# Wk's first load moves to ScalarE's DMA queue, and one transpose moves up, at the start of a two-layer transformer kernel

## The chip, the cores and the metric

The kernel runs on one core of a Trainium2 chip. A core has five engines that run side by side, each with its own instruction stream: TensorE (PE in the profile; its weight loads are PEld), VectorE (DVE), ScalarE (ACT), GpSimd (POOL) and SyncE (SP). They share an on-chip memory (SBUF) and an accumulation memory (PSUM), and wait for each other by semaphores. Sixteen DMA engines move data; SyncE, ScalarE and GpSimd can each issue transfers on a queue of their own. The metric is the device time of one execution in microseconds (us), as the median of several.

## What is computed

Two layers over 2048 tokens of 1024 features (bf16), the same weights in both: attention over eight keys at distances 0, 2, ..., 14, with 32 heads of 32 features, and a feed-forward part of 3584 hidden features. Each part stands behind a layer norm and is added to its input.

```python
def _A_ref(x, wqkv, wo):
    qkv = (x @ wqkv).reshape(B, S, 3, H, Dh).transpose(2, 0, 3, 1, 4)
    q, k, v = qkv[0], qkv[1], qkv[2]
    idx = pos[:, None] - (jnp.arange(8) * 2)[None, :]
    ...
    logits = jnp.where(mask, einsum("bhsd,bhswd->bhsw", q, kg) * scale, -1e9)
    o = einsum("bhsw,bhswd->bhsd", softmax(logits), vg)
    return o.transpose(0, 2, 1, 3).reshape(B, S, D) @ wo

def _B_ref(x, w1, b1, w2, b2):
    return gelu(x @ w1 + b1) @ w2 + b2

x = x + _A_ref(_layernorm(x), A_wqkv, A_wo)
x = x + _B_ref(_layernorm(x), B_w1, B_b1, B_w2, B_b2)
# and both lines once more
```

## The kernel before

The tokens are cut into four groups of 512 (four tiles of 128 tokens each), so that two layers make eight stages `n` = 0 to 7. A stage runs `gen_qkv` (queries, keys, values), the attention itself on VectorE (`new_prod`, `logits`, `weights`, `av`), `gen_wo` (output projection), `gen_ffn1` and `gen_ffn2`. The calls at the end of the kernel interleave the generators by hand; TensorE's order is the order in which they are written (`pe` chains every matmul to the one before). `InOrder` does the same for the other engines where its `on` flag is set. SyncE's flag is set from the load of group 1's first two tiles until the end of the first early layer norm, ScalarE's during the start of stage 0.

What matters here is the start of stage 0. The weights wqkv are loaded in three parts of 2 MB: Wq, Wk and Wv. Wk and Wv come as two halves of 1 MB each (`load_qkv`); the first Wq comes as eight rows of 256 KB (`load_wq_row`), shared out between the queues of SyncE and ScalarE together with the first four tiles of x. All weight halves share a ring of five buffers (`wpool`).

Stage 0 treats its first two token tiles unlike the others. TensorE transposes raw x of tiles 0 and 1 before the layer norm is known, and multiplies it with Wq row by row (`queries_of_raw`: for each row `k`, seven column chunks `c`, with an eighth chunk at the end); the norm is put in afterwards (`finish`, on VectorE and GpSimd). While this runs, `rest` computes the norm of tiles 2 and 3: VectorE's statistics (`stats`), a square root on ScalarE (`root`), then the normalised tiles (`norm`). Tiles 2 and 3 are transposed on TensorE between the rows, through one PSUM bank: tile 2 after place (6, 6), that is row 6, chunk 6, and tile 3 after place (7, 6); ScalarE copies each out of the bank (`transpose_on_pe`, `copy_transposed`). Tiles 0 and 1 are normalised as well, and their transposes for keys and values are done by two DMA transposes on SyncE.

After the rows TensorE computes the queries of tiles 2 and 3, then the keys of the whole group (eight chunks of eight matmuls; the first four use Wk's first half and the last four its second), then the values. SyncE issues in this order: tile 0 of x, Wq rows 0, 2, 3, tile 3, rows 5, 6, 7, group 1's tiles 0 and 1, the two DMA transposes, Wk's first half, group 1's tile 2, Wk's second half, group 1's tile 3, the four tiles of group 2, then the transposes of the early layer norm (`ln_early`) of group 1, and Wv. ScalarE issues tiles 1 and 2 and rows 1 and 4.

`ln_early` norms group 1 and the first tile of group 2 on VectorE, in two parts (two tiles, then three); `ln_stats_ahead` computes the statistics of the other tiles of group 2 on ScalarE and GpSimd during the keys.

Of the kernel before, what the change touches and what calls it, by code (L numbers as in the profile page):

```python
# [17 lines left out]
def kernel(  # L18
# [19 lines left out]
    _, S, D = A_x.shape  # L38
# [12 lines left out]
    KD = D // P  # L51
# [10 lines left out]
    wqkv_v = A_wqkv.rearrange("(k p) f -> p k f", p=P)  # L62
# [15 lines left out]
    def acc_tile():  # L78
        return psum.tile([P, T], F32, name="acc", bufs=8)
# [23 lines left out]
    vec, act, pool, sp = InOrder(nc.vector), InOrder(nc.scalar), InOrder(nc.gpsimd), InOrder(nc.sync)  # L103
# [17 lines left out]
    def load_x(g, t0=0, t1=NTT, engine=None):  # L121
        for tt in range(t0, t1):
            t = g * NTT + tt
            (engine or sp).dma_start(x[t][:], x_in[t * P:(t + 1) * P, :])

    def load_qkv(which, between=None, behind=None):
        tiles = []
        for h in range(2):
            wt = wpool.tile([P, KD // 2, D], BF16, name="wt")
            load = sp.dma_start(wt[:], wqkv_v[:, h * (KD // 2):(h + 1) * (KD // 2), which * D:(which + 1) * D])  # L130
            if h == 0 and behind:
                tc.add_manual_dep(load.ins, behind.ins.name,
                                  mybir.DependencyInfo(mybir.DependencyClass.Sync, mybir.DependencyReason.DATA),
                                  reason="behind the spread of the weights")
            if h == 0 and between:
                between()
            tiles.append(wt)
        return tiles

    def load_wq_row(k, engine):  # L140
        engine.dma_start(wq_first[k // (KD // 2)][:, k % (KD // 2), :], wqkv_v[:, k, 0:D])
# [3 lines left out]
    for k in (0, 2, 3):  # L145
        load_wq_row(k, sp)
    load_x(0, 3, 4)
    for k in range(5, KD):
        load_wq_row(k, sp)

    warm = bigp.tile([P, P], BF16, name="big")
# [8 lines left out]
    load_x(0, 1, 2, act)  # L160
    load_wq_row(1, act)
    load_x(0, 2, 3, act)
    load_wq_row(4, act)
    act.on = False
    ident = const.tile([P, P], BF16, name="ident")
    make_identity(nc, ident[:])
# [66 lines left out]
    def copy_transposed(out, bank, parts):  # L233
        pst = bank[:].bitcast(BF16).rearrange("p (k t) -> p k t", t=P)
        for k0, k1 in zip(parts[:-1], parts[1:]):
            act.copy(out[:, k0:k1, :], pst[:, k0:k1, :])
# [11 lines left out]
    def ln_first():  # L248

        xnT = xa[0] = new_xnT()  # L250
        vec.on = act.on = True
        raw = attp.tile([P, KD, NT + 2], BF16, name="vT", bufs=2)
        vec.memset(raw[:, :, NT:NT + 2], 1.0)
        mv = lnp.tile([P, 4, 2], F32, name="mvs", bufs=1)
        std = lnp.tile([P, 4], F32, name="stds", bufs=1)
        rstd = lnp.tile([P, 4], F32, name="rstds", bufs=1)
        less = lnp.tile([P, 2], F32, name="lesses", bufs=1)

        def stats(tt):
            st6 = lnp.tile([P, 2, 6], F32, name="stats")  # L260
            for h in range(2):
                vec.bn_stats(st6[:, h, :], x[tt][:, h * HALF:(h + 1) * HALF])
            vec.bn_aggr(mv[:, tt, :], st6[:])

        def root(t0, t1):
            act.activation(std[:, t0:t1], mv[:, t0:t1, 1], ACT.Sqrt, bias=eps_t[:])

        def norm(tt, out):
            if tt > 1:
                vec.reciprocal(rstd[:, tt:tt + 1], std[:, tt:tt + 1])  # L270
            vec.tensor_scalar(out=out, in0=x[tt][:], scalar1=mv[:, tt, 0:1], scalar2=rstd[:, tt:tt + 1],
                              op0=ALU.subtract, op1=ALU.mult)
            return out

        warm_ps = acc_tile()
        warm_up(7, warm_ps)
        banks = [acc_tile(), acc_tile()]
        for tt in range(2):
            transpose_on_pe(x[tt], raw[:, :, tt * P:(tt + 1) * P], banks[tt], (0, 2))
        warm_up(2, warm_ps)  # L280
        for tt in range(2):
            copy_transposed(raw[:, :, tt * P:(tt + 1) * P], banks[tt], (2, KD))
            stats(tt)
        root(0, 2)
        vec.tensor_scalar(out=less[:], in0=mv[:, 0:2, 0], scalar1=-1.0, scalar2=None, op0=ALU.mult)
        vec.reciprocal(rstd[:, 0:2], std[:, 0:2])
        by_token = iop.tile([P, 4, P], F32, name="tmp")

        def spread_stats(bank):
            for i, column in enumerate((less[:, 0:1], less[:, 1:2], rstd[:, 0:1], rstd[:, 1:2])):  # L290
                pe(nc.tensor.transpose(bank[:, i * P:(i + 1) * P], column.to_broadcast([P, P]), identf[:]))
            rows = by_token[:].rearrange("p i t -> p (i t)")
            act.copy(rows, bank[:])
            return rows[:, 0:NT], rows[:, NT:2 * NT]

        xn01 = bigp.tile([P, 2, D], BF16, name="big")

        def rest():
            for tt in range(2, 4):
                stats(tt)  # L300
                root(tt, tt + 1)
            for tt in range(2, 4):
                xn = lnp.tile([P, D], BF16, name="xn", bufs=3)
                norm(tt, xn[:])
                first_late.append((xn, xnT[:, tt, :, :]))
            for tt in range(2):
                first_early.append((norm(tt, xn01[:, tt, :]), xnT[:, tt, :, :]))

        return raw, spread_stats, rest

    def queries_of_raw(wq, qT):
        raw, spread_stats, rest = st.pop("raw")
        first = {}

        def row(c, k):
            if k == 0:
                first[c] = acc_tile()
            mm(first[c][:, 0:NT + 2], lhsT=wq[k // (KD // 2)][:, k % (KD // 2), c::NCH], rhs=raw[:, k, :],
               start=(k == 0), stop=(k == KD - 1), skip_group_check=True)

        part = attp.tile([P, NCH, NT], F32, name="abc")

        def finish(c):
            vec.scalar_tensor_tensor(out=part[:, c, :], in0=less, scalar=first[c][:, NT:NT + 1], in1=first[c][:, 0:NT],
                                     op0=ALU.mult, op1=ALU.add)
            pool.tensor_tensor(out=qT[:, c, 0:NT], in0=part[:, c, :], in1=rstd, op=ALU.mult)

        for k in range(KD):
            for c in range(7):
                row(c, k)  # L330
                if (k, c) == (0, 6):
                    bank = acc_tile()
                if (k, c) == (2, 6):
                    less, rstd = spread_stats(bank)
                    rest()
                if (k, c) == (6, 6):
                    transpose_on_pe(*first_late.pop(0), bank)
                if (k, c) == (7, 6):
                    transpose_on_pe(*first_late.pop(0), bank, (0, KD // 2, KD))
        act.on = False  # L340
        act.hold()
        for c in range(7):
            finish(c)
        for k in range(KD):
            row(7, k)
        vec.on = False
        return lambda: finish(7)

    def new_xnT(pool=None):
        return (pool or xnp).tile([P, NTT, KD, P], BF16, name="xnT")  # L350
# [38 lines left out]
    def gen_qkv(n, defer=False, qk_pool=None, v_late=False, qk_next=None, v_first=False, mix=0):  # L389
# [5 lines left out]
        if v_first:  # L395
            wv = load_qkv(2)
        wq = wq_first if n == 0 else load_qkv(0)
        if n > 0 and not v_first:
            wk = load_qkv(1, behind=last_spread[0] if n == 2 else None)
# [15 lines left out]
        if v_first:  # L415
            yield from values()
            wk = load_qkv(1)
        qT = qk_pool.tile([P, NCH, T], BF16, name="qT")
        if n == 0:
            last = queries_of_raw(wq, qT)  # L420
            for xn, out in first_early:
                sp.dma_start_transpose(out, xn.rearrange("s (k p) -> s k p", p=P))
            wk = load_qkv(1, lambda: load_x(1, 2, 3))
            load_x(1, 3, 4)
            load_x(2)
            early_tiles = ln_early((1, None), (2, qk_next))
            next(early_tiles)
            last()
            next(early_tiles)
            wv = load_qkv(2)  # L430
            for _ in early_tiles:
                pass
            vec.hold()
            sp.on = False
            sp.hold()
# [89 lines left out]
    def between(n, m):  # L525

        vec.on = True
        for c in range(2):
            new_prod(m, c, False)
        add_prods(m, 0)  # L530
        logits(n)
        add_prods(m, 1)
        weights(n)
        spread(n)
        new_prod(m, 2, False)
        add_prods(m)
        vec.on = False
# [101 lines left out]
    def warm_up(count, ps):  # L639
        for _ in range(count):  # L640
            mm(ps[:], lhsT=warm[:], rhs=warm[:].unsqueeze(1).to_broadcast([P, NTT, P]), start=True, stop=True)
# [135 lines left out]
```

## Time and profile before

| what | us |
|---|---|
| median of 5 executions | 1231.26 (1230.96 to 1231.49) |
| the profiled execution's own time | 1231.26 |
| its span, first to last instruction | 1229.5 |
| VectorE busy | 865.0 |
| ScalarE busy | 315.8 |
| DMA, mean rate | 185 GB/s |

Busy time is the time in which an engine ran an instruction of the kernel; DMA issues don't count. In a row of a timeline stand the start, the duration, the engine (a q behind it means its sequencer, which issues DMAs), the source line, the operation, the tile written and the tiles read, the shapes and the number of instructions merged into the row; in brackets the idle time of the engine ahead of it and what ended that. Nearly all rows have line L92 or L117, since helpers on those lines record every operation; the tile names tell them apart: `wt` is a weight half, `x` a token tile, `raw` (shown as vT) the raw transposed tiles, `xn` and `big` normalised tiles, `xnT` transposed ones, `acc` a PSUM bank. A row of a table by stretches has the stretch, its length, the busy time (and number of instructions) of PE, PEld, DVE, ACT and POOL, the granted clock, the share in which the DMA engines were busy, and their rate in GB/s.

The chain of waits that ended last goes, in its first part, through the loads of x and VectorE's statistics:

```profile
17.38 8.21 DMA x<-in_A_x_dram
25.58 0.02 issue
25.61 1.30 DVE stats L92 x2
```

### The profile page before, as it was taken

Reading aid. Unit: us, or ns where it says so; the run is one execution under the profiler, and the core shown is the slowest. Engines: PE = TensorE matmul, PEld = TensorE weight load, DVE = VectorE, ACT = ScalarE, POOL = GpSimd, SP = SyncE. Lnnn points to the kernel's source line nnn. Section 1 sums busy time; section 2 is a strip of 40 time slices with the busy share of each in tenths; the row PEclk is TensorE's granted clock in tenths of the full one; section 3 lists DMA queues with packets and bytes.
Section 4 is the critical chain, followed back from the end, with each engine's and each line's share of the span. In section 5 each row is a group of like instructions: output and inputs, shape, how many; then the busy total and the mean of one; then the engine's idle time right before and its main releaser. Section 6 shows DMA issues by size and latency. Waiting matters only on the chain.

```text
span 1229.5 us, 13975 instructions
## 1 busy us (share of the span) xinstructions
PE 1221.0 (99%) x5719; PEld 632.9 (51%) x5769; DVE 865.0 (70%) x922; ACT 315.8 (26%) x497; POOL 127.6 (10%) x220
## 2 busy tenths in 40 slices
PE   9999999999999999999999999999999999999998
PEld 7666544456444564445544465444654444444444
DVE  7999898998997999375993759937599797011001
ACT  4543253014410144202441024410244001400310
POOL 2630006010101101100001000010000002000000
PEclk9999999999999999999999999999999999999999
DMA  8966665766647645856447565476664568446441
GB/s 278 296 206 184 183 206 184 201 169 205 213 136 240 186 154 166 236 170 181 155 159 233 171 171 176 158 219 202 171 200 145 187 195 209 148 159 196 156 136 50
DMA packets 225824, 227.18 MB, mean 185 GB/s; under 512 B 74000, under 2 KB 192928, under 8 KB 223712
## 3 DMA queue, kind: packets, MB, share of 16 engines
q1 hardware_dynamic: 216304, 208.17, 56.1%
q0 software_dynamic: 8880, 17.07, 4.0%
q8 instruction: 45, 0.74, 0.3%
q10 hardware_dynamic: 576, 1.05, 0.2%
q14 instruction: 19, 0.16, 0.0%
HBM read 189.01 MB, written 4.19 MB: 157 GB/s over the span
## 4 chain that ended last, share of the span: by engine, by line
PE 90%; DVE 5%; POOL 1%; DMA 1%; issue 1%; ACT 0%; SPq 0%; DVEq 0%
PE acc L117 90%; DVE big L92 4%; POOL rstd_ahead L92 1%; DMA x<-in_A_x_dram 1%; DVE e L92 0%; DMA abc<-a 0%; POOL mv_ahead L92 0%; DVE tmp L92 0%; DVE stats L92 0%; DVE oT L92 0%; PE acc L230 0%; DVE abc L92 0%; SPq L92 0%; POOL abc L92 0%; ACT xn L92 0%
## 5 line engine op out<-in xcount | busy, mean ns | idle before, releaser
L117 PE MATMUL acc<-xnT,wt 128*128 128x512 bf16 (+1 forms) x3328 | 713.2, 377 | 1.3 <-DMA wt<-in_A_wqkv_dram 1.3
L117 PEld LDWEIGHTS <-wt 128*128 128x128 bf16 x3392 | 400.7, 119 | 319.7 <-DMA wt<-in_A_wqkv_dram 1.7
L117 PE MATMUL acc<-wt,hT 128*128 128x512 bf16 (+1 forms) x1780 | 386.0, 376 | 2.1
L117 PEld LDWEIGHTS <-hT 128*128 128x128 bf16 x1820 | 178.1, 98 | 208.9
L92 DVE TENSOR_TENSOR big<-big 128x2048 bf16<-128x2048 bf16 (+2 forms) x185 | 245.2, 1355 | 2.2
L92 ACT ACTIVATE hT<-acc,b1T 128x512 bf16<-128x512 f32 x224 | 151.8, 689 | 323.7 <-PE acc L117 323.6
L92 DVE TENSOR_TENSOR big<-qT,kT 128x4096 bf16<-128x4096 bf16 x64 | 144.0, 2287 | 37.2 <-ACT kT L92 35.9
L92 DVE TENSOR_TENSOR big<-abc,vT 128x4096 bf16<-128x4096 bf16 x64 | 144.8, 2288 | 9.9 <-DMA abc<-a 7.4
L92 DVE TENSOR_TENSOR tmp<-acc,b2bc 128x512 f32<-128x512 f32 x56 | 38.7, 691 | 156.1 <-PE acc L117 152.9
L92 ACT CAST qT<-acc 128x512 bf16<-128x512 f32 (+1 forms) x64 | 35.6, 558 | 278.7 <-PE acc L117 277.0
L117 PE MATMUL acc<-wt,oT 128*128 128x512 bf16 x440 | 97.6, 379 | 0.4
L92 DVE BATCH_NORM_STATS2 stats<-x 128x6 f32<-128x512 bf16 x114 | 76.3, 682 | 7.2 <-DMA x<-in_A_x_dram 6.2
L117 PEld LDWEIGHTS <-oT 128*128 128x128 bf16 x448 | 43.8, 98 | 53.0 <-DVE oT L92 0.3
L92 DVE TENSOR_TENSOR x<-acc,big 128x512 bf16<-128x512 f32 (+1 forms) x9 | 5.7, 632 | 90.0 <-PE acc L117 90.0
L92 POOL TENSOR_TENSOR rstd<-mv,eps_t 128x1 f32<-128x1 f32 x48 | 14.6, 304 | 501.1 <-DVE mv L92 501.1
L92 ACT CAST vT<-acc 128x512 bf16<-128x512 f32 x64 | 37.4, 585 | 100.1 <-PE acc L117 100.1
L92 ACT CAST kT<-acc 128x512 bf16<-128x512 f32 x64 | 37.0, 585 | 59.9 <-PE acc L117 59.9
L92 DVE TENSOR_TENSOR x<-acc,x 128x512 bf16<-128x512 f32 x64 | 43.0, 671 | 4.9 <-PE acc L117 4.6
L92 DVE TENSOR_SCALAR xn<-x,mv,rstd 128x1024 bf16<-128x1024 bf16 x48 | 26.2, 547 | 19.9 <-POOL rstd L92 19.9
L92 DVE TENSOR_TENSOR x<-tmp,x 128x512 bf16<-128x512 f32 x56 | 38.7, 691 | 1.4
L92 POOL DMA_DIRECT2D big<-big x24 | 13.3, 564 | 212.3 <-DVE big L92 212.3
L92 ACT ACT_TABLE_LOAD x17 | 21.8, 1283 | 41.9 <-DVE e L92 28.9
(82 smaller groups left out, 312.9 us busy)
## 6 DMA issues: line engine op xcount, KB each, us to landing
wt<-in_B_w_dram SPq DMA_DIRECT2D x56, 1024.0 KB, 5.6
wt<-in_B_w_dram SPq DMA_DIRECT2D x64, 896.0 KB, 4.8
wt<-in_A_wqkv_dram SPq DMA_DIRECT2D x46, 1024.0 KB, 5.6
wt<-in_A_wo_dram SPq DMA_DIRECT2D x16, 1024.0 KB, 5.1
abc<-a POOLq DMA_DIRECT2D x32, 256.0 KB, 4.9
big<-big POOLq DMA_DIRECT2D x24, 256.0 KB, 3.8
out_dram<-x SPq DMA_DIRECT2D x31, 128.0 KB, 1.8
x<-in_A_x_dram SPq DMA_DIRECT2D x14, 256.0 KB, 5.9
```

The costliest lines, as they stand in the source:

```text
L92: inst = f(*args, **kwargs)
L117: return pe(nc.tensor.matmul(*args, **kwargs))
```

## The change

Three things. Both halves of Wk are issued by ScalarE, directly behind the square root of tile 2, in place of SyncE; the loads of group 1's tiles 2 and 3, which stood between and behind the halves, follow SyncE's two DMA transposes directly. Row 4 of Wq goes from ScalarE's queue to SyncE's, between tile 3 and row 5. And the transposes of tile 2 on TensorE stand after place (6, 1) instead of (6, 6). Nothing of the computation changes.

```diff
-    def load_qkv(which, between=None, behind=None):
+    def load_qkv(which, behind=None, engine=None):
         tiles = []
         for h in range(2):
             wt = wpool.tile([P, KD // 2, D], BF16, name="wt")
-            load = sp.dma_start(wt[:], wqkv_v[:, h * (KD // 2):(h + 1) * (KD // 2), which * D:(which + 1) * D])
+            load = (engine or sp).dma_start(wt[:], wqkv_v[:, h * (KD // 2):(h + 1) * (KD // 2), which * D:(which + 1) * D])
...
-            if h == 0 and between:
-                between()
...
     load_x(0, 3, 4)
-    for k in range(5, KD):
+    for k in range(4, KD):
         load_wq_row(k, sp)
...
     load_x(0, 2, 3, act)
-    load_wq_row(4, act)
     act.on = False
...
-        def rest():
+        def rest(load_wk):
             for tt in range(2, 4):
                 stats(tt)
                 root(tt, tt + 1)
+                if tt == 2:
+                    load_wk()
...
                     less, rstd = spread_stats(bank)
-                    rest()
-                if (k, c) == (6, 6):
+                    rest(load_wk)
+                if (k, c) == (6, 1):
                     transpose_on_pe(*first_late.pop(0), bank)
...
         if n == 0:
-            last = queries_of_raw(wq, qT)
+            wk = []
+            last = queries_of_raw(wq, qT, lambda: wk.extend(load_qkv(1, engine=act)))
             for xn, out in first_early:
                 sp.dma_start_transpose(out, xn.rearrange("s (k p) -> s k p", p=P))
-            wk = load_qkv(1, lambda: load_x(1, 2, 3))
-            load_x(1, 3, 4)
+            load_x(1, 2, 4)
             load_x(2)
```

More of the change, by code (lines that the diff above doesn't have):

```diff
@@ L309, in ln_first, with queries_of_raw @@
         return raw, spread_stats, rest
-    def queries_of_raw(wq, qT):
+    def queries_of_raw(wq, qT, load_wk):
         raw, spread_stats, rest = st.pop("raw")
```

## The prediction

> **What bounds the kernel now.** I read the page's busy times first, then the chain of waits, then TensorE's waits, then the timelines of the first 30 us.
>
> ```profile
> PE 1221.0 (99%) x5719; PEld 632.9 (51%) x5769; DVE 865.0 (70%) x922; ACT 315.8 (26%) x497; POOL 127.6 (10%) x220
> ```
>
> TensorE (PE) is busy 1221.0 of 1229.5 us, so the end moves only by what TensorE stops losing, or begins to lose. Its waits after the first 5 us are two:
>
> ```profile
> PE acc L117 <- DMA wt<-in_A_wqkv_dram: 1.3, 1, 1.3
> PE acc L230 <- ACT xnT L92: 0.3, 1, 0.3
> ```
>
> TensorE's timeline places them:
>
> ```profile
> 12.60 0.61 PE L230 MATMUL acc<-ident,xn 128*128 128x128 bf16 x8
> 13.04 0.94 PE L117 MATMUL acc<-vT,wt 128*128 128x258 bf16 x7
> 14.31 0.61 PE L230 MATMUL acc<-ident,xn 128*128 128x128 bf16 x8 [0.32 <-ACT xnT L92]
> ...
> 15.66 8.01 PE L117 MATMUL acc<-xnT,wt 128*128 128x256 bf16 x68
> 24.95 2.38 PE L117 MATMUL acc<-xnT,wt 128*128 128x512 bf16 x10 [1.28 <-DMA wt<-in_A_wqkv_dram]
> ```
>
> The first wait stands before the transposes of tile 3: they use the PSUM bank that ScalarE is still copying tile 2 out of. The second is Wk's second half, which the key matmuls need from their fifth on. Ends are modelled, so I price the waits by the pitch of the starts. A row matmul takes 0.110 us (13.04 plus seven slots is 13.82), and tile 3 starts at 14.31: 0.48 us lost. The 64 half-width queries run at 0.109 us from 15.66 to 22.65, four key matmuls at 0.216 (99.34 us for 460 in the stretch 24.95 to 124.29) follow, and the fifth should start at 23.51 instead of 24.95: 1.44 us lost, and some 0.06 more, since the ten restarted ones take 2.38 instead of 2.32. Together 1.98 us. From there TensorE runs without a wait to the output projection at 124.29.
>
> Why Wk is late is seen on SyncE's queue and in the DMA rate:
>
> ```profile
> 12.89 2.79 SPq L92 DMA_TRANSPOSE xnT<-big  x2
> 15.73 0.57 SPq L92 DMA_DIRECT2D wt<-in_A_wqkv_dram  x1
> 16.36 0.50 SPq L92 DMA_DIRECT2D x<-in_A_x_dram  x1
> 16.90 0.43 SPq L92 DMA_DIRECT2D wt<-in_A_wqkv_dram  x1
> 17.38 3.21 SPq L92 DMA_DIRECT2D x<-in_A_x_dram  x5
> ```
>
> ```profile
> 12.30:14.00 1.70, 1.69 (x20) 1.50 (x19) 1.66 (x5) 0.76 (x1) 0.00 (x0) 1.00 0.04 13
> 14.00:17.00 3.00, 2.69 (x29) 2.69 (x29) 3.00 (x8) 1.60 (x4) 2.99 (x5) 1.00 0.78 177
> 18.00:27.00 9.00, 7.72 (x59) 6.48 (x57) 5.89 (x14) 3.07 (x8) 2.06 (x4) 1.00 1.01 371
> ```
>
> The last two columns are the DMA share and GB/s. The Wk loads stand behind two DMA transposes that wait for VectorE, and the DMA engines are empty for 1.7 us. Then all is asked for at once: the second half of Wk lands 8.0 us after its issue, at 24.9.
>
> [...] from 3 to 8 us the queues of SyncE and ScalarE moved 1.14 and 0.84 MB, 396 GB/s together. How packets of 256 B (transposes) and 2 KB (weights) on two queues share, no stretch of this trace shows. [...] here they reach about 290 GB/s in their best slices against 371 to 396. [...] tiny GpSimd steps take 1.5 to 2.7 us while VectorE runs products of 2.3 us.
>
> **The change part by part.**
>
> *Tile 2 one place sooner.* The eight transposes move ahead of five row matmuls, to 9.51 + 23 x 0.110 = 12.04. Their input is normalised at 11.21 + 0.55 = 11.76. The copy (1.01 us, from 13.24) goes 0.55 up: 12.69 to 13.70. Tile 3 can then start at 13.76 (now 0.05 after the copy), and its slot is 13.82: the 0.48 us goes, by a margin of 0.06. All behind it, tile 3's copies included, follow on.
>
> *One Wq row to SyncE.* ScalarE issued it at 4.21, and was idle till 5.31; nothing is won there. SyncE is idle from 3.34 to 5.54 and has room. The same bytes precede the row in either queue, so it lands near 9.6 as now (4.21 + 5.4); it is used at 9.51 + 7 x 0.110 = 10.28. Zero. If a row came late, TensorE would wait that much; the last one lands at 7.24 + 4.5 = 11.7, and is used at 13.04.
>
> *Wk on ScalarE.* Two issues of about 0.45 us (0.38 to 0.45 for ScalarE's others, 0.43 and 0.57 for these on SyncE) behind the root at 10.20; the next root is at 11.18. ScalarE's issues can run beside its compute (its first load went out at 0.91 during a table load from 0.74 to 2.02), so the root slips by 0 to 0.3 us; I take 0.1. Behind it stand recip and norm of tile 3 on VectorE (needed by TensorE at 13.82, ready at 12.4), and the first two transposes: no loss.
>
> The data start about 1.1 us after the issue, near 11.4, beside the end of group 1's first two tiles. Counted from 12.3, with some 0.2 MB of Wk done: 1.9 MB at 390 GB/s are 4.9 us, the two transposes (0.53 MB) 1.8 to 2.4[...]: everything by about 20.1, landed 20.5. [...] The keys now want the transposed tiles at 22.65 - 0.48 = 22.17 and Wk's second half at 23.03. Both are ahead, the first by 1.6 us: the 1.50 us goes too. If transposes came first, they would land at 17 to 18; the far end is under rival C.
>
> *x loads.* Six of 0.26 MB follow the transposes: first landed about 21.5, then one each 0.67 us, the third 22.9, the last 24.9 (now 20.15 + 8.3 = 28.5). VectorE now waits for them:
>
> ```profile
> 22.23 1.29 DVE L92 BATCH_NORM_STATS2 stats<-x 128x6 f32<-128x512 bf16 x2 [1.07 <-DMA x<-in_A_x_dram]
> ...
> 25.61 1.29 DVE L92 BATCH_NORM_STATS2 stats<-x 128x6 f32<-128x512 bf16 x2 [1.84 <-DMA x<-in_A_x_dram]
> ```
>
> Three tiles of 1.4 us from 21.5 end at 25.7 instead of 28.53, so VectorE's chain comes 2.8 us sooner, 2 if SyncE is held longer issuing the transposes. ScalarE's statistics (from 29.23) follow the second key copy and the root, both sooner by 2.0 to 2.8; GpSimd's steps end with VectorE's products, so they go along.
>
> *What is late next.* TensorE reaches the output projection 1.98 us sooner, 122.31. VectorE's last oT is done at 124.30 + 0.77 = 125.07, and the eighth matmul now starts at 125.99, 124.01 then: VectorE must gain about 1.3. It has 2 to 2.8. The projection's second half of weights, issued at 120.17, lands 5.1 later at 125.3 and holds TensorE some 0.19; its buffer is freed by TensorE, so it moves along. Wv's second half lands at 29.00 + 8.8 = 37.8 and is used at 38.83, in future 36.85; it is issued after the x loads and two transposes, which all come some 3 us sooner.
>
> Sum: 0.48 + 1.50 = 1.98. The profiled execution took 1231.26 us (span 1229.5 and 1.8 around it), exactly the median of the runs shown: 1231.26 - 1.98 = 1229.28.
>
> **The rivals.**
>
> A, both stalls go: 1229.3; chance 0.70.
>
> B, VectorE takes over. If the x loads don't come sooner (SyncE held in its transposes), the oT stay at 125.07 and the eighth matmul starts near 125.3: 0.7 gained, 1230.6. For it: in the loaded stretch from 21.60 two transposes hold SyncE for 6.68 us. Against: what they stand behind there is 3 MB, here it is gone by 19. Chance 0.10.
>
> C, slower: the transposes starve beside Wk. Place: xnT of tiles 0 and 1. At 14.0 about 1.43 MB of Wk are left, 44 packets for each engine. In the trace a 2 KB packet takes 86 ns and a 256 B one 18, but 92 to 123 in a bad stretch from 36.0 to 37.0. [...] Keys then start 2.85 late, net 0.87 slower: 1232.1. It decides when the transposes land after 22.17 + 1.98 = 24.15. For it: no trace of this mixture, and transposes took 3.6 to 4.2 us to issue under load. Against: the work is conserved, and 290 GB/s unloaded. Chance 0.11.
>
> D, it does only half: the copy's margin of 0.06 is missed or a new wait stands at tile 3; 0.48 stays: 1229.8. Chance 0.09.
>
> **How the numbers follow.** About 0.2% (2.46 us) is what a measurement of this kernel can tell from no change: below 1228.80 or above 1233.72. A needs another half microsecond that TensorE doesn't lose anywhere (0.19 at most): 0.08 faster. C would have to be three times as bad: 0.08 slower. Within: 0.84. The range 1228.8 to 1231.2 leaves C and A's far tail out; A alone spans 1228.9 to 1229.9.
>
> **What would show it.** TensorE's waits: neither of the two lines left. Tile 3's transposes near 13.82, keys from 22.2 without a gap, the projection at 122.3. Wk landed by 19, xnT by 20.5, VectorE's statistics done near 25.7. Wrong if a key matmul waits for xnT, or the projection for oT.

## The result, and the profile after

The kernel after takes 1228.66 us (median of 22 executions, 1228.29 to 1229.40) against 1231.26 for the kernel before (42 executions): ratio 0.9978, 95% interval 0.9972 to 0.9983. That is 2.60 us less, where 1.98 were forecast; it lies 0.14 us below the stated range, and just over the prediction's bound of 0.2%.

The page of the kernel after, busy times first, then the chain of waits by engine:

```profile
PE 1219.9 (99%) x5719; PEld 632.0 (52%) x5769; DVE 865.0 (71%) x922; ACT 315.4 (26%) x497; POOL 127.9 (10%) x220
...
PE 99%; issue 0%; DVE 0%
```

TensorE's waits, over the whole span (who waited for what, us in total, times, longest):

```profile
PE acc L117 <- DVE vT L92: 1.0, 1, 1.0
```

That one is the start of the program. Both waits of the kernel before are gone, and the chain, which went through other engines, VectorE above all, and the loads of x for a tenth of the span, is now TensorE for 99% of it. TensorE's timeline at the same places:

```profile
4.16 1.28 PE L227 MATMUL acc<-ident,x 128*128 128x128 bf16 x16
5.28 0.59 PE L117 MATMUL acc<-big 128*128 128x512 bf16 x2
5.90 2.52 PE L117 MATMUL acc<-vT,wt 128*128 128x258 bf16 x21
...
11.43 0.62 PE L227 MATMUL acc<-ident,xn 128*128 128x128 bf16 x8
11.89 1.49 PE L117 MATMUL acc<-vT,wt 128*128 128x258 bf16 x12
13.22 0.61 PE L227 MATMUL acc<-ident,xn 128*128 128x128 bf16 x8
13.66 1.07 PE L117 MATMUL acc<-vT,wt 128*128 128x258 bf16 x8
14.57 11.68 PE L117 MATMUL acc<-xnT,wt 128*128 128x256 bf16 x85
```

Tile 3's transposes follow without a wait, and queries and keys run on as one row. But more has changed than the two waits: the rows of raw x begin at 5.90 instead of 6.76, and the queries at 14.57, 1.09 us sooner, where the moved transposes account for 0.48. The first row shows why: sixteen transposes took 1.28 us here and 1.89 in the first profile of before. TensorE starts at half speed (the warm-up matmuls of 512 columns stand 0.42 us apart, the keys' matmuls of that size 0.216), and in this execution its clock record shows full speed from 4.04 us on, in that one from 6.74. I call that moment the clock step. So the two profiled executions differ in something that the change doesn't touch. The experiments ask whether this difference belongs to the effect.

VectorE's statistics and the DMA rates went as follows (for the second view: the stretch, its length, busy PE, PEld, DVE, ACT, POOL, granted clock, DMA share, GB/s):

```profile
21.96 1.29 DVE L92 BATCH_NORM_STATS2 stats<-x 128x6 f32<-128x512 bf16 x2 [1.19 <-DMA x<-in_A_x_dram]
...
24.80 1.23 DVE L92 BATCH_NORM_STATS2 stats<-x 128x6 f32<-128x512 bf16 x2
26.07 0.21 DVE L92 BATCH_NORM_AGGREGATE mv<-stats 128x2 f32<-128x12 f32 x1
```

```profile
12.30:14.00 1.70, 1.70 (x21) 1.69 (x20) 1.70 (x5) 0.93 (x2) 0.51 (x1) 1.00 1.05 394
14.00:16.50 2.50, 2.50 (x25) 2.50 (x24) 2.50 (x7) 1.31 (x3) 2.50 (x5) 1.00 1.04 383
16.50:19.00 2.50, 2.50 (x25) 2.50 (x24) 2.42 (x7) 1.17 (x4) 1.94 (x4) 1.00 1.17 218
19.00:21.00 2.00, 2.00 (x20) 2.00 (x19) 1.70 (x4) 0.99 (x4) 0.84 (x2) 1.00 1.24 258
```

The hole of 12.3 to 14.0 (13 GB/s before) is filled by Wk, and the statistics end 2.2 us sooner.

### The profile page after: what moved, and what is told of

Its sections match the earlier page's. It is cut to its first block, busy times and chain, and to the rows that moved or that the text cites. A ratio compares the mean times of both kernels' runs of the same rounds, so it can differ in the third digit from the quotient of the medians.

```text
span 1226.7 us, 13976 instructions
## 1 busy us (share of the span) xinstructions
PE 1219.9 (99%) x5719; PEld 632.0 (52%) x5769; DVE 865.0 (71%) x922; ACT 315.4 (26%) x497; POOL 127.9 (10%) x220
## 4 chain that ended last, share of the span: by engine, by line
PE 99%; issue 0%; DVE 0%
PE acc L117 99%; PE acc L227 0%; PE acc L288 0%; DVE x L92 0%; DVE big L92 0%; DVE vT L92 0%
## 5 line engine op out<-in xcount | busy, mean ns | idle before, releaser
L92 DVE TENSOR_SCALAR xn<-x,mv,rstd 128x1024 bf16<-128x1024 bf16 x48 | 26.2, 547 | 19.9 <-POOL rstd L92 19.7
```

The lines of the kernel that those rows point to most:

```text
L92: inst = f(*args, **kwargs)
```

## The experiments

Theory S (slack): in the kernel before, Wk's landing fixes where the keys go on; whatever TensorE gains or loses ahead of it, a clock step included, goes into the wait. In the kernel after nothing catches it. The gain is then not the wait of one execution, but each execution's own. Theory L (later): the surplus, the 0.6 us beyond the forecast 1.98, comes from behind the keys. The third reading is the prediction's, a sum of single gains.

### The two parts alone, and both kernels again

The transposes of tile 2 alone:

```diff
-                if (k, c) == (6, 6):
+                if (k, c) == (6, 1):
```

> Only the transposes of tile 2 at place (6, 1). Theory S: the wait at tile 3 goes (0.48 us), the queries start sooner by it, and the wait for Wk grows by as much: 1231.2, no change (within 0.2). A sum of single gains, as the prediction made it, gives 1230.8. Rival L: also 1230.8.

Measured 1231.54 against 1231.56 for the kernel before beside it: ratio 1.0001 (0.9993 to 1.0009). The part that the prediction booked at 0.48 us gives nothing by itself. Its profile shows the transposes of tile 3 without their wait, and two waits for Wk:

```profile
13.33 0.61 PE L230 MATMUL acc<-ident,xn 128*128 128x128 bf16 x8
...
22.14 1.08 PE L117 MATMUL acc<-xnT,wt 128*128 128x512 bf16 x4 [0.31 <-DMA wt<-in_A_wqkv_dram]
25.50 6.72 PE L117 MATMUL acc<-xnT,wt 128*128 128x512 bf16 x24 [2.29 <-DMA wt<-in_A_wqkv_dram]
```

Not all of the longer wait is the change's: this execution has an early clock step (4.38), and it is one of those whose clock fell back later, which come below.

Wk on ScalarE alone (the change without the two other parts):

```diff
-    for k in range(4, KD):
+    for k in range(5, KD):
         load_wq_row(k, sp)
...
     load_wq_row(1, act)
     load_x(0, 2, 3, act)
+    load_wq_row(4, act)
...
-                if (k, c) == (6, 1):
+                if (k, c) == (6, 6):
```

> Only Wk on ScalarE's queue; tile 2 stays at (6, 6) and row 4 on ScalarE. Theory S: all of the gain but the 0.48 at tile 3, 2.6 - 0.5 = 2.1: 1229.1. The sum of single gains: 1.50, 1229.8. Rival L: 1229.8 if the extra 0.6 hangs on the row or tile 2, 1229.1 if on Wk; then the start of the fifth key matmul (near 22.9) tells.

Measured 1229.24: ratio 0.9978 (0.9970 to 0.9986), 2.32 us less, against 1.50 by the sum. The whole change beside it gives 2.79, and the difference, 0.47, is the size of the 0.48 of tile 3: it counts only once the wait behind it is gone. The two gains themselves are a little large, since 12 of the 39 executions of the kernel before in this series have the fall of the clock described below (above 1232.4 us, with a mean granted clock of 0.998 or 0.999; the other 27 have 1.000); against the median of the other 27, 1231.19, Wk alone gains 1.95 and the whole change 2.42, still more than 1.50 and 1.98. The fifth key matmul of the profiled execution starts at 23.61, later than the 22.9 I gave, since its clock step was late (7.02) and the queries started at 15.76.

> The kernel after once more: 1228.7, ratio 0.998. Theory S: if the clock steps late (past 6 us), queries start near 15.2 and keys near 22.2, and this one execution takes about 1229.2; if early, 14.6 and 21.6, and about 1228.5. Rival L: the time doesn't follow the step.

Measured 1228.77, ratio 0.9977 (0.9968 to 0.9986). The profiled execution stepped at 4.92 and took 1228.66: early, and near what was expected. Its keys began at 21.69, 0.28 us behind the last query in place of 0.11; the transposes of tiles 0 and 1 had landed at 21.55. So here TensorE waited 0.17 us for xnT.

> The kernel before once more. Every theory: 1231.2, ratio 1.000. What is looked for is the moment at which TensorE's clock steps up (6.74 us in the first profile of before, 4.04 in that of after). Theory S (slack): the fifth key matmul starts when Wk's second half lands, near 24.9, whatever that moment is; a profile with an early step shows TensorE at the queries some 0.5 us sooner and at the keys no sooner. Rival L (later): the 0.6 us beyond the forecast 1.98 come from behind the keys, and an early step makes this kernel faster too.

Measured 1231.59, ratio 1.000 (0.9992 to 1.0008). Its profile, TensorE's timeline:

```profile
4.10 1.89 PE L230 MATMUL acc<-ident,x 128*128 128x128 bf16 x16
5.78 0.68 PE L117 MATMUL acc<-big 128*128 128x512 bf16 x2
6.45 2.52 PE L117 MATMUL acc<-vT,wt 128*128 128x258 bf16 x21
...
15.38 8.01 PE L117 MATMUL acc<-xnT,wt 128*128 128x256 bf16 x68
24.99 1.30 PE L117 MATMUL acc<-xnT,wt 128*128 128x512 bf16 x5 [1.60 <-DMA wt<-in_A_wqkv_dram]
```

The step came at 5.94, 0.8 us sooner than in the first profile; the queries start 0.28 us sooner (15.38), the fifth key matmul at 24.99 instead of 24.95, and the wait grew from 1.28 to 1.60. That is the slack at work. L fails on the time behind the keys. An execution's time less the start of its fifth key matmul is 1206.12 us here, 1206.14 in two further profiles of before and 1206.05 to 1206.10 in all five of the kernel after (the table below has the figures). The first profile of before has 1206.31; there TensorE loses 0.19 us in the output projection, the loss that the prediction named. So some 0.1 us of the gain comes from behind the keys, not 0.6.

Row 4 of Wq alone:

```diff
-    for k in range(5, KD):
+    for k in range(4, KD):
         load_wq_row(k, sp)
...
-    load_wq_row(4, act)
```

> Only row 4 of Wq on SyncE's queue. The prediction: nothing, 1231.2. Theory S: the same. Were the row the source of the 0.6 us beyond the forecast: 1230.6.

Measured 1231.16 against 1231.29, ratio 0.9997 (0.9988 to 1.0005): nothing that can be told, as forecast.

### TensorE made slower

Sixteen more transposes of tile 3, in both kernels, write the same values twice more ahead of the queries:

```diff
                 if (k, c) == (7, 6):
+                    again = bank[:].bitcast(BF16).rearrange("p (k t) -> p k t", t=P)
+                    for i in range(2 * KD):
+                        xn = first_late[0][0]
+                        pe(nc.tensor.transpose(again[:, i % KD, :], xn[:, i % KD * P:(i % KD + 1) * P], ident[:]))
                     transpose_on_pe(*first_late.pop(0), bank, (0, KD // 2, KD))
```

> The kernel before with tile 3's transposes written three times in place of once: 16 more on TensorE, 16 x 0.0555 = 0.89 us, ahead of the queries; the result is the same. Theory S (slack): the wait for Wk (1.5 us and more) shrinks by 0.89 and the keys go on at 24.95: 1231.3 as before, and the executions near 1233.2 become rarer or go, since they are those in which TensorE's clock falls back to half during a long wait. Rival (a TensorE microsecond counts everywhere): 1232.2.

> The kernel after with the same 16 transposes added. Theory S: no wait is left to take them, 1228.7 + 0.9 = 1229.6. If some slack is left before the keys: between 1228.7 and 1229.6.

Before with the extra work: 1231.29 against 1231.19 for the kernel before beside it, ratio 0.9997 (0.9989 to 1.0005; it is no ratio of the medians, and the executions with a fall of the clock, described below, weigh on it). After with it: 1229.47 (ratio 0.9983, 0.9977 to 0.9990). The kernel after did not run in this series: 1229.47 is 0.7 to 0.8 us above its medians elsewhere, and the gain over the kernel before beside it is 1.72 in place of 2.60 to 2.79. The same work is free, within 0.2 us, in one kernel and counts about in full in the other. The profile of the slowed kernel before shows the work and the smaller wait:

```profile
13.62 1.05 PE L342 MATMUL acc<-ident,xn 128*128 128x128 bf16 x16 [0.32 <-ACT xnT L92]
...
15.86 8.01 PE L117 MATMUL acc<-xnT,wt 128*128 128x256 bf16 x68
24.98 1.30 PE L117 MATMUL acc<-xnT,wt 128*128 128x512 bf16 x5 [1.10 <-DMA wt<-in_A_wqkv_dram]
```

The keys go on at 24.98, though the clock step was early (4.97). And of its 13 executions none is above 1232.4, while 14 of 57 of the kernel before beside it are.

The second way to slow TensorE takes four of the seven warm-up matmuls from its start:

```diff
-        warm_up(7, warm_ps)
+        warm_up(3, warm_ps)
```

> The kernel before with three warm-up matmuls at the start in place of seven[...]. Theory S: TensorE comes to the queries 1 to 2 us later, within the wait for Wk: 1231.3 to 1231.8, and no executions near 1233.2. Rival: 1232.5 to 1233.

> The kernel after with three warm-up matmuls in place of seven. Theory S: the late start counts nearly in full, 1 to 1.8 us: 1229.7 to 1230.5. If the start-up phase doesn't matter: 1228.7.

After: 1229.91 (ratio 0.9988, 0.9982 to 0.9995), as S expected, and the executions spread over 3.0 us (1228.84 to 1231.84). Before: 1232.45 (ratio 1.0008, 1.0000 to 1.0016), 1.3 us more: my expectation missed, and so S in its strict form. The clock fell back in none of these 13 (mean granted clock 1.000 in each), as expected; the 1.3 us are something else. The profile says what was overlooked, ScalarE's timeline first for the kernel before, then for this one:

```profile
9.71 0.59 ACT L92 COPY tmp<-acc 128x512 f32<-128x512 f32 x1 [1.59 <-PE acc L291]
10.20 0.29 ACT L92 ACTIVATE stds<-mvs,eps_t 128x1 f32<-128x1 f32 x1
```

```profile
10.65 0.59 ACT L92 COPY tmp<-acc 128x512 f32<-128x512 f32 x1 [2.69 <-PE acc L291]
11.13 0.48 ACT L92 ACTIVATE stds<-mvs,eps_t 128x1 f32<-128x1 f32 x2
```

Wk's place behind SyncE's transposes hangs on the norms of tiles 0 and 1, these stand behind tile 2's root on VectorE, and the root stands on ScalarE behind the copy of the spread norms, which TensorE (L291) makes. With TensorE 0.9 us later there (the copy starts at 10.65 in place of 9.71), the root slips from 10.20 to 11.13. It had some half microsecond to spare ahead of VectorE's next step (11.06), so the two transposes are issued 0.45 us later, at 13.34 in place of 12.89. Wk's second half lands at 26.2, some 1.25 us later: another 0.6 comes from the issue of the transposes itself, which held SyncE for 3.39 us in place of 2.79. In the six profiles of the kernel before it held it for 2.68 to 3.30; whether the later start made it longer here is not shown. So Wk's landing is free of TensorE only within some half microsecond; beyond, it goes along.

### Single executions

> The kernel after, one more look, to pair the moment of the clock step with the time of that very execution. Theory S: step before 5.5 us, queries near 14.5 and about 1228.6; step after 6.3, queries from 14.9 to 15.2 and 1229.0 to 1229.4. Rival: no relation.

> As the look before: an early step (before 5.5 us) gives about 1228.6, a late one (after 6.3) 1229.0 to 1229.4.

> As the look before: an early step (before 5.5 us) gives about 1228.6, a late one (after 6.3) 1229.0 to 1229.4.

> The kernel before, one more look, for the clock step and the time of the same execution. Theory S in its strict form: the fifth key matmul starts at 24.9 to 25.0 and the execution takes 1231.1 to 1231.3 whatever the step. Theory S in a loose form: Wk's landing follows TensorE's start a little (ScalarE's copy of the spread norms stands ahead of the root), so that an early step (before 5 us) gives 24.5 and 1230.8. Rival: early steps give 1230.6 or less, as in the kernel after.

> As the look before: strict 24.9 to 25.0 and 1231.1 to 1231.3; loose, with an early step, 24.5 and 1230.8; or an execution near 1233.2, and then TensorE's clock is at half for 3.4 us from within the wait for Wk on.

> As the look before: strict 24.9 to 25.0 and 1231.1 to 1231.3; loose, with an early step, 24.5 and 1230.8; or near 1233.2 with the clock at half for 3.4 us.

> As the look before: strict 24.9 to 25.0 and 1231.1 to 1231.3; loose, with an early step, 24.5 and 1230.8; or near 1233.2 with the clock at half for 3.4 us.

All profiled executions of the two kernels, by the step of the clock (us from the span's start; "keys" is the start of the fifth key matmul, which needs Wk's second half):

| kernel | clock step | queries | keys | time |
|---|---|---|---|---|
| after | 4.04 | 14.57 | 22.42 | 1228.47 |
| after | 4.29 | 14.49 | 22.34 | 1228.42 |
| after | 4.92 | 14.54 | 22.58 | 1228.66 |
| after | 5.78 | 14.85 | 22.70 | 1228.80 |
| after | 7.04 | 15.24 | 23.09 | 1229.18 |
| before | 4.85 | 15.05 | 24.98 | 1232.78, clock fell back |
| before | 5.58 | 15.23 | 25.28 | 1233.27, clock fell back |
| before | 5.83 | 15.52 | 25.26 | 1231.40 |
| before | 5.94 | 15.38 | 24.99 | 1231.11 |
| before | 6.29 | 15.45 | 24.96 | 1231.10 |
| before | 6.74 | 15.66 | 24.95 | 1231.26 |

The kernel after follows the step: 0.7 us from the earliest to the latest (at 4.92 with the 0.17 us for xnT in it). The kernel before doesn't: its keys go on at 24.95 to 25.28 in no order of the step. They go with SyncE instead: the two latest, 25.26 and 25.28, are those in which the transposes held it longest (2.90 and 3.30 us). The strict form of S is too strict all the same. The profile of the kernel with row 4 alone moved, with a step at 4.60, has the transposes issued at 12.40, the keys at 24.51 and a time of 1230.83, as the loose form has it; the kernel before with a step at 4.85 has 12.72 and 24.98.

In three executions with early steps (4.38, 4.85 and 5.58 us) something worse happens. TensorE's timeline and the stretches of the execution that took 1233.27:

```profile
15.23 8.01 PE L117 MATMUL acc<-xnT,wt 128*128 128x256 bf16 x68
25.28 7.09 PE L117 MATMUL acc<-xnT,wt 128*128 128x512 bf16 x24 [2.03 <-DMA wt<-in_A_wqkv_dram]
```

```profile
22.30:26.00 3.70, 1.67 (x9) 0.85 (x8) 1.56 (x4) 0.37 (x1) 0.00 (x0) 1.00 1.05 384
26.10:29.40 3.30, 3.30 (x10) 1.29 (x9) 2.85 (x7) 0.88 (x2) 0.00 (x0) 0.50 1.14 267
29.50:33.00 3.50, 3.50 (x18) 2.29 (x16) 3.43 (x6) 3.16 (x6) 1.46 (x1) 1.00 1.01 276
```

The last column but two is the granted clock: 0.50 for 3.41 us, from 26.06 on, which is 0.8 behind the end of the wait. Ten matmuls stand in the middle stretch and eighteen in the next. The eight matmuls lost, 8 x 0.216 = 1.7 us, are the distance from 1231.4 to 1233. Three profiled executions have this: the two marked in the table, with waits of 1.92 and 2.03 us, and that of the tile 2 kernel, 1232.94, with a wait of 2.29; none of the kernel after has it. Of the kernel before, 7 of 42 executions lie above 1232.4 (12 of 39, 14 of 57 and 6 of 17 in the other series); of the kernel after none of 33.

No faster version than the kernel after was tried. Between TensorE's first row and 30 us its longest pause is the one for xnT above, 0.17 us; ahead of the first row stands one of some 0.2.

## Why the prediction was wrong

The direction and the mechanism held, and the size was too small by 0.62 us.

*The step that failed* is the price of the second wait: "the fifth should start at 23.51 instead of 24.95: 1.44 us lost". 23.51 is right for the execution on the page, in which TensorE's clock had stepped up at 6.74, the latest of the six executions of this kernel. In the five others TensorE reaches that place sooner. Priced in the same way their waits are 1.66, 1.75, 1.89, 2.07 and 2.19 us, and the mean of all six is 1.83 where I had 1.44; I took one execution's wait for the kernel's. At a like, late step the forecast is good: 1231.26 (6.74) less 1229.18 (7.04) is 2.08. With the early steps, 4.04 to 4.92, the kernel after takes 1228.42 to 1228.66, and the undisturbed times of before stay at 1231.1 to 1231.4: 2.4 to 3.0. The sixteen transposes at 1.89 us were in the profile; read against their later fellows (eight in 0.61), they would have told that this execution stayed long at half speed.

*The sum 0.48 + 1.50* took the two waits as independent, and they are not: alone, the first is worth 0 and the Wk part 2.32, together they are 2.79. That did not make the forecast wrong, since both waits went; for one of them alone it would have.

*Tile 2 sooner, row 4, ScalarE's issues.* As forecast: tile 3's wait went, the row costs and brings nothing, and the two Wk issues took 0.95 us on ScalarE's queue while the root at 9.41 ran, with no root late for them.

*Transposes and x loads.* Of the right kind, and later than I worked out. Wk's second half landed at 19.56 (near 19 forecast), the transposes at 20.3 and 21.25 (20.5), the first x load at 21.94 (21.5), the statistics ended at 26.3 (25.7). SyncE was held 5.83 us by the two issues, the worse of the two cases that I had named. The margin ahead of the keys is 0.3 us in place of 1.6, and with TensorE sooner, in the second profile of after, tile 1 landed at 21.55 and the keys began at 21.69, 0.17 late: the sign of being wrong that the prediction named, a key matmul that waits for xnT, in one profile of five and at a sixth of a microsecond. C's 2.85 us took for granted how two queues share the DMA engines, as did Wk near 19; both were estimates of mine, with no trace behind that part, as was half a microsecond of the 20.1 for everything. And C was not what happened: small packets took 18 ns (median) from 16.5 to 18.5 beside Wk too, but before 16.5 none ran. C's 92 to 123 ns were means of a stretch in which most small packets took 18 ns and a few about a microsecond. B did not come: VectorE's last oT was done at 122.37, forecast near 122.3, ahead of its matmul.

*The chances.* I called 0.84 for within 0.2% because I knew no place where TensorE lost more. The fall of the clock, which makes the wait for Wk cost 1.7 us more in a sixth to a third of the executions, was not in the forecast either. It hardly moves the median of the 42 (without those seven executions it is 1231.22), but the mean by 0.3 us (1231.48 with them, 1231.17 without); where 12 of 39 have it, the median moves by 0.37 too. So it is a small part of the 2.60. The longer waits are the larger one of what was missing: 0.48, 1.83 and 0.06 make 2.37. The last 0.2 I can't place; the profiled executions are few, and their steps differ between the kernels.

## What to carry to other kernels

The length of a wait in one profile is that execution's; ask what each of its two ends hangs on, and if one hangs on a DMA transfer and the other on an engine, price it over the range of that engine's arrivals. Gains ahead of a wait on the same engine are worth nothing until that wait is gone, as long as its end doesn't move with them, and they count afterwards. A long wait can have a second price, seen only in some executions: here the granted clock fell to 0.50 for 3.41 us at waits of 1.92, 2.03 and 2.29 us, and at none of six waits of 1.10 to 1.73.

## What the runs showed of the hardware

With seven warm-up matmuls, TensorE's step to full speed came at any time from 3.67 us (the kernel after with the extra transposes) to 7.04, a spread of 3.37, in sixteen profiled executions with the same start at 0.99 or 1.00. From that step to the next fall of the clock it was 20.48 us in each of the three executions with a fall within the kernel (from 5.58 to 26.06 in the one shown above), and 1221.97 us in the first profiles of before and after, whose fall stands at the end of the kernel. The two are 6 and 358 times 3.413 us; in all traces whose first fall is the one at the end, the time is 352 to 359 times that length. Each of the three falls lasted 3.41 us. What sets this length, and the moment of the step, the runs don't show. The 3.41 us ahead of the three falls held 1.91, 1.94 and 2.03 us without a matmul. In seven other executions, with stretches of the same length counted on from the step, the one with most of the wait for Wk held 1.10 to 1.73 us without a matmul, and the clock stayed (ends of matmuls are modelled). The wait of 2.29 us ended after its fall had begun; 1.65 of it lay ahead of the fall.

Two DMA transposes beside a weight load on another queue got almost nothing: with the first issued at 12.5, they moved no data until 16.5, when 0.37 of Wk's 2.1 MB were left. Without that load, in the kernel before, data followed the issue at 12.9 by some 1.3 us. While both ran (16.5 to 19.0) the rate fell to 218 GB/s, from 383 to 394. How the prediction let the two queues share the DMA engines was an estimate that this stretch doesn't bear out; whether the queue or something ahead of it held the transposes stays open.
